# Gate products on centred tokens, with the scale in the eviction, and whole-slab transposes in a sequence layer

## The chip, the cores and the metric

The kernel runs on one core of a Trainium2 chip. The metric is the device time in microseconds (us) of a run. The time before is the median of three runs. The profile is of one further execution.

## The reference

Only what matters is kept. `x` has 2048 tokens of 512 features in bf16.

```python
xn = (x - mean(x)) / sqrt(var(x) + 1e-5)                  # per token
# A: a diagonal complex recurrence over the 2048 tokens
Bu = xn @ B_bar.T                                         # complex, 512 states
h[t] = Lam_bar * h[t-1] + Bu[t]
s = 2 * real(h @ Cmat.T) + xn * Dskip
# B: a gated feed-forward network, F = 1376
g = silu((gelu(xn @ w_gate) * (xn @ w_up)) @ w_down)
out = x + s * g
```

The normalisation divides each token by its own standard deviation. A product with a weight matrix is linear in the token, so `xn @ w` equals `rstd * ((x - mean) @ w)`.

## The kernel before

The tokens go in four slabs of 512, each of four tiles of 128 tokens. All engines run lists that a scheduler in the kernel has ordered beforehand; each engine works its list strictly in order. The order of TensorE for slab 0 is: gate and up products of chunk 0 (384 columns) for the four tiles, chunk 1 (512 columns), the state products of the slab, chunk 2 (480 columns). Then come the state products of slab 1, the down product of slab 0, the gate tiles of slab 1, between them the y tiles of slab 0, and so on.

```python
    # the queue on SyncE, in this order
    load_x(SP, nc.sync, 0, 1.75)
    load_x(SP, nc.sync, 1, 1.9)
    load_first(0, 0, 2.1)            # w_gate chunk 0
    load_x(SP, nc.sync, 2, 2.55)
    load_first(0, 1, 3.1)            # w_up chunk 0
    load_x(SP, nc.sync, 3, 2.9)
    load_first(1, 0, 3.5)            # w_gate, w_up chunk 1
    load_first(1, 1, 3.5)
    dma_first(SP, ...)               # x_tok of slab 1, 512 KB
    for ri, src in enumerate((A_B_re, A_B_im)):      # B, turned on the way
        dma_first(SP, ..., nc.sync.dma_start_transpose(out=BT[:, ri, :, :], in_=src), ...)
    # w_gate, w_up chunk 2, then w_down ...
```

A tile of slab 0 is normalised on VectorE, turned by TensorE into a PSUM bank and evicted. The inverse deviation `rs` comes from a power on GpSimd.

```python
    def norm_dve(s, m):
        V.tensor_scalar(out=xn[m][:], in0=x_tok[:, s * M + m, :],
            scalar1=mv[:, s, m, 0:1], scalar2=rs[:, s, m : m + 1],
            op0=ALU.subtract, op1=ALU.mult)

    def transposed(src, n, dst, reads, writes, bank, evict):
        ...                                     # four T.transpose into ybank[bank]
        if evict == ACT:
            act(out=dst, in_=tp, func=AF.Copy)
        else:
            V.tensor_copy(out=dst, in_=tp)

    def gate_pair(s, m, c, then=((), ()), spare=False):
        ...                                     # one PSUM slot (two banks), or both ybanks
        for bank, (nm, wt) in enumerate((("wg", wg), ("wu", wu))):
            for k in range(KT):
                T.matmul(pss[bank][:, 0:w], lhsT=xnT[:, k, t0 : t0 + P], rhs=wt[:, k, a:b], ...)
        act(out=ud, in_=pss[1][:, 0:w], func=AF.Copy)
        act(out=gd, in_=pss[0][:, 0:w], func=AF.Gelu_apprx_tanh)
        V.tensor_tensor(out=at[j][:, a:b], in0=gd, in1=ud, op=ALU.mult)
```

There are three such slots. ScalarE also loads the table for the sines right after the exponential of `log_dt`, makes the sines and cosines of the rotation tables, and spreads `Dskip` over the partitions (`Drow`).

Slab 1 is normalised on VectorE too, and turned by four DMA transposes of one tile each (`dma_t`). The y tiles multiply states by `C2`, made on VectorE from the turned C matrices, and add the skip term:

```python
    def y_part(s, m, bank, key, a, z, i, e, gi, b, seed):
        if seed:                                # all but the first two y tiles
            act(out=bank, in_=sk[s % 2][:, m, a:z], func=AF.Copy)
        ...                                     # eight matmuls onto the bank
        if seed:
            V.tensor_tensor(out=yg[e][:, a:z], in0=bank, in1=g2[gi][:, b, a:z], op=ALU.mult)
        else:
            V.tensor_tensor(out=ys, in0=bank, in1=sk[s % 2][:, m, :], op=ALU.add)
            V.tensor_tensor(out=yg[e][:], in0=ys, in1=g2[gi][:, b, :], op=ALU.mult)
```

Of the kernel before, what the change touches and what calls it, by code (L numbers as in the profile page):

```python
# [19 lines left out]
LOOK, HOLD, TABLE, ROUNDS, TRIALS = 0.3, 8.0, 6.0, 6, 3000  # L20
# [182 lines left out]
def kernel(  # L203
# [50 lines left out]
    xnT = sb("xnT", [P, KT, 2 * TS])  # L254
# [20 lines left out]
    xn = [sb(f"xn{i}", [P, D]) for i in range(M)]  # L275
# [5 lines left out]
    tF = sb("tF", [P, 2, D], FP32)  # L281
    junk = sb("junk", [P, D])
# [31 lines left out]
    def dma_first(eng, issue, land, emit, writes, **kw):  # L314

        first[eng] = dma(eng, issue, land, emit, writes=writes, after=[first[eng]] if eng in first else (), **kw)
# [29 lines left out]
    dma_first(SP, 1.45, 4.0, lambda: nc.sync.dma_start(out=x_tok[:, M : 2 * M, :], in_=x_r[:, M : 2 * M, :]), [("x", 1, m) for m in range(M)])  # L346
    for ri, src in enumerate((A_B_re, A_B_im)):
        dma_first(SP, 2.4, 4.0, lambda ri=ri, src=src: nc.sync.dma_start_transpose(out=BT[:, ri, :, :], in_=src), [("BT", ri)])
    for which in range(2):
        load_w(dma_first, SP, nc.sync, 2, (1.35, 4.1), which)  # L350
# [21 lines left out]
    def columns():  # L372

        pe(1, 150, lambda: T.matmul(rows, lhsT=pv[0][:], rhs=ident[0 : 2 * NPT, 0 : 2 * NPT], start=True, stop=True),
            [("pv", 0), ("pv", 1), "ident"], [("slot", 2, 0)])
        acts(4, lambda: act(out=dt_, in_=rows[:, 0:NPT], func=AF.Exp), [("slot", 2, 0), "tiny"], ["dt"], table="exp", rank=150.0)
        acts(1, lambda: act(out=tiny[:], in_=zero[:], func=AF.Sin), ["zero", "dt"], ["tiny"], table="silu", rank=150.0)
# [44 lines left out]
    def transposed(src, n, dst, reads, writes, bank, evict):  # L422
        tp = ybank[bank][:].bitcast(BF16)[:, 0:D].rearrange("p (k t) -> p k t", t=P)

        def f():
            for k in range(KT):
                T.transpose(tp[:, k, :], src[:, k * P : (k + 1) * P], ident[:])  # L427
        pe(KT, P, f, reads + ["ident"], [("y", bank)])
        if evict == ACT:
            acts(512, lambda: act(out=dst, in_=tp, func=AF.Copy), [("y", bank)], writes, rank=100.0)  # L430
        else:
            dve(512, lambda: V.tensor_copy(out=dst, in_=tp), [("y", bank)], writes, rate=2.0, rank=40.0)
# [10 lines left out]
    def norm_dve(s, m):  # L443
        dve(512, lambda: V.tensor_scalar(  # L444
            out=xn[m][:], in0=x_tok[:, s * M + m, :], scalar1=mv[:, s, m, 0:1], scalar2=rs[:, s, m : m + 1],
            op0=ALU.subtract, op1=ALU.mult), [("x", s, m), ("mv", s, m), ("rs", s, m)], [("xn", m)], rate=2.0)

# [3 lines left out]
    def dma_t(s, m):  # L451
        c0 = (s % 2) * TS + m * P
        return dma(SP, 1.2, 4.5 if s == 1 else 1.3, lambda: nc.sync.dma_start_transpose(out=xnT[:, :, c0 : c0 + P], in_=xn[m][:]),
            [("xn", m)], turned_tile(s, m))

    def skip(s, m):
        dve(512, lambda: V.tensor_tensor(out=sk[s % 2][:, m, :], in0=xn[m][:], in1=Drow[:], op=ALU.mult),
            [("xn", m), "Drow"], [("sk", s % 2, m)], rate=2.0)
# [4 lines left out]
    def gate_pair(s, m, c, then=((), ()), spare=False):  # L463

        if spare:
            pss, both = [ybank[0][:], ybank[1][:]], [("y", 0), ("y", 1)]
        else:
            i, ps = slot()
            pss, both = [ps[:, 0, :], ps[:, 1, :]], [("slot", i, 0), ("slot", i, 1)]
        a, b = CH0[c]  # L470
        w = b - a
        j = (s * M + m) % NAT
        t0 = (s % 2) * TS + m * P
        q = gu_n[0] % (2 * NGT)
        gu_n[0] += 1
        qb, qo = q // 2, (q % 2) * 512
        for bank, (nm, wt) in enumerate((("wg", wg), ("wu", wu))):
            def f(bank=bank, wt=wt):
                for k in range(KT):
                    T.matmul(pss[bank][:, 0:w], lhsT=xnT[:, k, t0 : t0 + P], rhs=wt[:, k, a:b], start=(k == 0), stop=(k == KT - 1))  # L480
            pe(KT, w, f, turned_tile(s, m) + [(nm, c)], [both[bank]])
            for t in then[bank]:
                t()
        gd, ud = gt[qb][:, qo : qo + w], ub[qb][:, qo : qo + w]
        acts(w, lambda: act(out=ud, in_=pss[1][:, 0:w], func=AF.Copy), both, [("ub", q)])
        acts(w, lambda: act(out=gd, in_=pss[0][:, 0:w], func=AF.Gelu_apprx_tanh), both, [("gt", q)], table="gelu", after=early if c == 0 else (), rank=40.0 if c + m == 0 else 0.0)
        dve(w, lambda: V.tensor_tensor(out=at[j][:, a:b], in0=gd, in1=ud, op=ALU.mult), [("gt", q), ("ub", q)], [("at", j, c)], rate=2.0)

    def gate_tile(s, m):

        j = (s * M + m) % NAT
        t0 = (s % 2) * TS + m * P
# [3 lines left out]
        def mm(ps, bank, wt, c):  # L496
            a, b = CH[c]

            def f():
                for k in range(KT):  # L500
                    T.matmul(ps[:, bank, 0 : b - a], lhsT=xnT[:, k, t0 : t0 + P], rhs=wt[:, k, a:b], start=(k == 0), stop=(k == KT - 1))  # L501
# [51 lines left out]
    def y_tile(s, m):  # L553
        i = y_n[0] % 2
        seed = y_n[0] >= 2
# [7 lines left out]
        for bank, key, a, z in parts:  # L563
            y_part(s, m, bank, key, a, z, i, e, gi, b, seed)

    def y_part(s, m, bank, key, a, z, i, e, gi, b, seed):

        w = z - a
        if seed:
            acts(w, lambda: act(out=bank, in_=sk[s % 2][:, m, a:z], func=AF.Copy), [("sk", s % 2, m)], [key])  # L570

        def f():
            for j in range(2 * NPT):
                T.matmul(bank, lhsT=hst[s % 2][:, j // NPT, j % NPT, m * P : (m + 1) * P], rhs=C2[:, j // NPT, j % NPT, a:z],  # L574
                         start=(j == 0 and not seed), stop=(j == 2 * NPT - 1), skip_group_check=True)
        pe(2 * NPT, w, f, [("hst", s % 2, 0), ("hst", s % 2, 1)] + C2S + ([key] if seed else []), [key])
        if seed:
            dve(w, lambda: V.tensor_tensor(out=yg[e][:, a:z], in0=bank, in1=g2[gi][:, b, a:z], op=ALU.mult),  # L578
                [key, ("g2", gi)], [("yg", e, a)], base=0.13)
        else:  # L580
            ys = tF[:, i, :]
            dve(512, lambda: V.tensor_tensor(out=ys, in0=bank, in1=sk[s % 2][:, m, :], op=ALU.add),
                [key, ("sk", s % 2, m)], [("tF",)], base=0.13)
            dve(512, lambda: V.tensor_tensor(out=yg[e][:], in0=ys, in1=g2[gi][:, b, :], op=ALU.mult),
                [("tF",), ("g2", gi)], [("yg", e, a)], base=0.13)
# [16 lines left out]
    def half(s, h):  # L602
# [3 lines left out]
        for q in range(H2):  # L606
            i, ps = slot()
            pt = h * H2 + q
            for ri in range(2):
                def f(ri=ri, pt=pt, ps=ps):  # L610
                    for k in range(KT):
                        T.matmul(ps[:, ri, :], lhsT=BT[:, ri, k, pt * P : (pt + 1) * P], rhs=xnT[:, k, (s % 2) * TS : (s % 2 + 1) * TS],  # L612
# [61 lines left out]
    def tables():  # L674
# [5 lines left out]
        for f32, lo, pr, n in ((cbt, ch, cp, "c"), (sbt, sh, sp, "s")):  # L680
            pool(0.5, lambda f32=f32, lo=lo: G.tensor_copy(out=lo[:], in_=f32[:, :, 0:NB]), [n + "bt"], [n + "h"])
            acts(128, lambda f32=f32, pr=pr: act(
                out=pr[:], in_=f32[:, :, NB : NB + NA].unsqueeze(3).to_broadcast([P, NPT, NA, 2]), func=AF.Copy), [n + "bt"], [n + "p"], rank=40.0)
# [28 lines left out]
    def head_t(m):  # L712
        transposed(xn[m], m, xnT[:, :, m * P : (m + 1) * P], [("xn", m)], [("xnT", 0, m)], m % 2, DVE if m == 3 else ACT)

    def spread():
        pe(1, 512, lambda: T.matmul(slots[2][:, 1, :], lhsT=warm[0:1, 0:P], rhs=Drow[0:1, :], start=True, stop=True), ["Drow", "warm"], [("slot", 2, 1)])
        acts(512, lambda: act(out=Drow[:], in_=slots[2][:, 1, :], func=AF.Copy), [("slot", 2, 0), ("slot", 2, 1)], ["Drow"])
# [3 lines left out]
    dummies(3, 0)  # L721
# [3 lines left out]
    rstd(0, 0, 1)  # L725
    stats(0, 1)
    mean(0, 1)
    norm_dve(0, 0)
    rstd(0, 1, 2)
    head_t(0)  # L730
    dummies(2, 0, 3)
    turn_angles()
    angle(0)
    norm_dve(0, 1)
    stats(0, 2)
    mean(0, 2)
    rstd(0, 2, 3)
    angle(1)
    stats(0, 3)
    norm_dve(0, 2)  # L740
    mean(0, 3)
    rstd(0, 3, 4)
    angle(2)
    angle(3)
    norm_dve(0, 3)
    pl.in_turn = False
    tables()
    then = {0: ((lambda: head_t(1), spread), ()), 1: ((lambda: head_t(2),), ()), 2: ((lambda: head_t(3),), ())}
    for m in range(M):
        gate_pair(0, m, 0, then.get(m, ((), ())), m == M - 1)  # L750
        if m == 1:
            damping()
    dma_first(SP, 3.6, 4.3, lambda: nc.sync.dma_start(out=wd[:, 0 : NFT - 1, :], in_=B_w_down[0 : (NFT - 1) * P, :].rearrange("(k p) d -> p k d", p=P)), ["wd"])
    dma_first(SP, 0.4, 4.3, lambda: nc.sync.dma_start(out=wd[:FL, NFT - 1, :], in_=B_w_down[(NFT - 1) * P : F, :]), ["wd"])
    for m in range(M):
        skip(0, m)
    for m in range(M):
        gate_pair(0, m, 1)
    for h in range(2):
        half(0, h)  # L760
    for m in range(M):
        gate_pair(0, m, 2)
# [38 lines left out]
    turned = {}  # L801

    def norm_out(s, m):
        acts(512, lambda: act(out=xn[m][:], in_=x_tok[:, s * M + m, :], func=AF.Identity, scale=rs[:, s, m : m + 1], bias=nb[:, s, m : m + 1]),
             [("x", s, m), ("rs", s, m), ("nb", s)], [("xn", m)], ptr=2)
        dma_t(s, m)

    def norm1():
# [4 lines left out]
        for m in range(M):  # L813
            norm_dve(1, m)
            turned[1] = dma_t(1, m)
            skip(1, m)

    def norm_act(s):
        dma(SP, 0.5, 4.0, lambda: nc.sync.dma_start(out=x_tok[:, s * M : (s + 1) * M, :], in_=x_r[:, s * M : (s + 1) * M, :]),
            writes=[("x", s, m) for m in range(M)], not_before=30.0)  # L820
# [19 lines left out]
    for ri, src in enumerate((A_C_re, A_C_im)):  # L840
        dma(SP, 2.4, 5.0, lambda ri=ri, src=src: nc.sync.dma_start_transpose(out=CT[:, ri, :, :], in_=src),
            writes=[("CT", ri)], after=[turned[1]])
# [68 lines left out]
```

## Time and profile before

| what | value |
|---|---|
| time, median of 3 | 181.07 us (181.01 to 181.15) |
| span of the profiled execution | 179.6 us |
| TensorE busy | 97% |
| VectorE busy | 88% |
| ScalarE busy | 65% |
| packets of the main DMA queue, share of 16 engines | 46.3% |
| granted TensorE clock | 0.998 |

A line of the timeline names its start and length in us, the engine, the line of the kernel, the operation, what is written and read, the shape, the count, and in brackets how long the engine sat idle before it and what ended that. "SPq" is SyncE's queue: its length is the time to issue a transfer, not to move the data. Lines of the chain of waits have start, length and what the time went to. One warning: matmuls overlap, so the step from one group to the next says more than a group's own length. A DMA transpose to SBUF counts as a transfer.

### The profile page before, as it was taken

What the parts mean: (1) busy time and instruction counts of PE and PEld (TensorE: products, weight loads), DVE (VectorE), ACT (ScalarE), POOL (GpSimd) and SP (SyncE); (2) the same over time, 40 slices, a digit from 0 to 9 for tenths busy, and PEclk for the clock granted to TensorE, in tenths of its full rate; (3) what the DMA queues carried; (4) which work ended last, traced back from release to release, by engine and by line L of the source; (5) the groups of instructions that cost most, each with busy time, mean ns of one, the idle gap of its engine ahead of it and who ended that gap; (6) DMA issues with size and microseconds to landing.
All of it is one profiled execution on the core that took longest, in us unless ns stands there. A gap on an engine that the chain in (4) does not pass through costs nothing.

```text
span 179.6 us, 2392 instructions
## 1 busy us (share of the span) xinstructions
PE 173.4 (97%) x838; PEld 82.6 (46%) x854; DVE 157.8 (88%) x268; ACT 116.7 (65%) x178; POOL 9.7 (5%) x19
## 2 busy tenths in 40 slices
PE   7999999999999999999999999999999999999992
PEld 2354444444445555444445554544445555444451
DVE  4789999998999999999999999999999999950063
ACT  4788599589999999645359964426618666353220
POOL 3230230000002000000020000000000000000000
PEclk9999999999999999999999999999999999999999
DMA  4999999997000429630011485050100084420011
GB/s 127 332 285 218 367 202 179 305 156 155 0 0 0 80 57 114 130 61 0 0 60 62 93 155 109 1 111 4 58 29 0 2 160 84 82 86 29 0 58 58
DMA packets 47109, 18.01 MB, mean 100 GB/s; under 512 B 38425, under 2 KB 47098, under 8 KB 47098
## 3 DMA queue, kind: packets, MB, share of 16 engines
q1 hardware_dynamic: 47072, 17.86, 46.3%
q8 instruction: 6, 0.10, 0.2%
q14 instruction: 5, 0.04, 0.1%
q10 hardware_dynamic: 26, 0.00, 0.0%
HBM read 6.33 MB, written 2.10 MB: 47 GB/s over the span
## 4 chain that ended last, share of the span: by engine, by line
PE 90%; DMA 4%; DVE 2%; SPq 1%; issue 1%; DVEq 0%
PE slot L501 31%; PE slot L544 21%; PE slot L612 15%; PE ybank L574 13%; PE slot L480 9%; DMA x_tok<-in_A_x_dram 3%; DMA out_dram<-ot 1%; DVE ot L586 1%; PE ybank L480 1%; SPq L328 1%; DVE yg L578 1%; SPq L321 1%; DVE st L402 0%; PE ybank L427 0%; DVE xn L444 0%
## 5 line engine op out<-in xcount | busy, mean ns | idle before, releaser
L501 PEld LDWEIGHTS <-xnT 128*128 128x128 bf16 x288 | 28.2, 98 | 28.4
L544 PE MATMUL slot<-wd,atT 128*128 128x512 bf16 (+1 forms) x173 | 38.5, 379 | 0.2
L501 PE MATMUL slot<-wu,xnT 128*128 128x512 bf16 (+1 forms) x144 | 31.8, 357 | 0.0
L501 PE MATMUL slot<-wg,xnT 128*128 128x512 bf16 (+1 forms) x139 | 31.5, 356 | 0.3
L645 DVE TENSOR_TENSOR_SCAN Fs<-rho,ini,W 128x512 bf16<-128x512 f32 x24 | 29.4, 1269 | 0.0
L612 PE MATMUL slot<-xnT,BT 128*128 128x512 bf16 x124 | 28.1, 379 | 0.2
L574 PE MATMUL ybank<-C,hst 128*128 128x512 bf16 (+1 forms) x125 | 27.6, 372 | 0.2
L544 PEld LDWEIGHTS <-atT 128*128 128x128 bf16 (+1 forms) x176 | 17.2, 98 | 20.9
L615 ACT ACTIVATE U<-slot 128x1024 bf16<-128x1024 f32 x16 | 16.0, 1021 | 12.5 <-PE slot L612 12.5
L578 DVE TENSOR_TENSOR yg<-ybank,g 128x512 bf16<-128x512 f32 (+1 forms) x14 | 9.4, 670 | 12.8 <-PE ybank L574 12.5
L574 PEld LDWEIGHTS <-hst 128*128 128x128 bf16 x136 | 13.3, 98 | 13.8
L612 PEld LDWEIGHTS <-BT 128*128 128x128 bf16 x128 | 12.5, 98 | 15.1
L626 DVE TENSOR_TENSOR Q<-U,tab 128x4096 bf16<-128x4096 bf16 x8 | 18.3, 2289 | 0.2
L626 DVE TENSOR_TENSOR Q<-Fs,tab 128x4096 bf16<-128x4096 bf16 x8 | 18.3, 2289 | 0.1
L548 ACT ACTIVATE g<-slot 128x1024 f32<-128x1024 f32 x8 | 8.2, 1021 | 13.4 <-PE slot L544 13.4
L570 ACT ACTIVATE ybank<-sk 128x512 f32<-128x512 bf16 (+1 forms) x14 | 8.1, 586 | 12.7 <-DVE yg L578 12.0
L509 ACT ACTIVATE gt<-slot 128x1024 bf16<-128x1024 f32 x12 | 12.3, 1023 | 3.7 <-PE slot L501 3.7
L509 ACT ACTIVATE ub<-slot 128x1024 bf16<-128x1024 f32 x12 | 12.2, 1020 | 3.0 <-PE slot L501 2.8
L480 PEld LDWEIGHTS <-xnT 128*128 128x128 bf16 x96 | 9.0, 98 | 9.7 <-ACT xnT L430 0.7
L823 ACT ACTIVATE junk<-x_tok 128x512 bf16<-128x512 bf16 x16 | 10.0, 627 | 1.6 <-DMA x_tok<-in_A_x_dram 1.4
L480 PE MATMUL slot<-wg,xnT 128*128 128x480 bf16 (+2 forms) x43 | 10.4, 360 | 0.4 <-ACT xnT L430 0.4
L480 PE MATMUL slot<-wu,xnT 128*128 128x512 bf16 (+2 forms) x44 | 10.4, 360 | 0.0
(118 smaller groups left out, 179.1 us busy)
## 6 DMA issues: line engine op xcount, KB each, us to landing
out_dram<-ot SPq DMA_DIRECT2D x15, 128.0 KB, 1.7
x_tok<-in_A_x_dram SPq DMA_DIRECT2D x3, 512.0 KB, 5.8
wd<-in_B_w_down_dram SPq DMA_DIRECT2D x1, 1280.0 KB, 9.9
x_tok<-in_A_x_dram SPq DMA_DIRECT2D x4, 128.0 KB, 3.0
wg<-in_B_w_gate_dram SPq DMA_DIRECT2D x1, 512.0 KB
wu<-in_B_w_up_dram SPq DMA_DIRECT2D x1, 512.0 KB, 6.9
wg<-in_B_w_gate_dram SPq DMA_DIRECT2D x1, 480.0 KB, 5.0
wu<-in_B_w_up_dram SPq DMA_DIRECT2D x1, 480.0 KB
```

What stands on the lines that cost most here:

```text
L480: T.matmul(pss[bank][:, 0:w], lhsT=xnT[:, k, t0 : t0 + P], rhs=wt[:, k, a:b], start=(k == 0), stop=(k == KT - 1))
L501: T.matmul(ps[:, bank, 0 : b - a], lhsT=xnT[:, k, t0 : t0 + P], rhs=wt[:, k, a:b], start=(k == 0), stop=(k == KT - 1))
L509: acts(1024, lambda ps=ps, dst=dst, fn=fn: act(out=dst[:, 0:1024].rearrange("p (c w) -> p c w", c=2), in_=ps[:, :, :], func=fn), [("slot", ...
L544: T.matmul(ps[:, b, :], lhsT=atT[:fs, k, m * P : (m + 1) * P], rhs=wd[:fs, k, :], start=(k == 0), stop=(k == NFT - 1))
L548: acts(1024, lambda: act(out=g2[gi][:, :, :], in_=ps[:, :, :], func=AF.Silu), [("slot", i, 0), ("slot", i, 1)], [("g2", gi)], table="silu" ...
L574: T.matmul(bank, lhsT=hst[s % 2][:, j // NPT, j % NPT, m * P : (m + 1) * P], rhs=C2[:, j // NPT, j % NPT, a:z], start=(j == 0 and not seed ...
L578: dve(w, lambda: V.tensor_tensor(out=yg[e][:, a:z], in0=bank, in1=g2[gi][:, b, a:z], op=ALU.mult), [key, ("g2", gi)], [("yg", e, a)], base ...
L612: T.matmul(ps[:, ri, :], lhsT=BT[:, ri, k, pt * P : (pt + 1) * P], rhs=xnT[:, k, (s % 2) * TS : (s % 2 + 1) * TS], start=(k == 0), stop=(k ...
L615: acts(1024, lambda q=q, ps=ps: act(out=U[ui][:, :, q, :], in_=ps[:, :, :], func=AF.Copy), [("slot", i, 0), ("slot", i, 1)], [("U", ui, q)])
L626: dve(4096, lambda: V.tensor_tensor(out=Qf, in0=src.unsqueeze(1).to_broadcast(WQ), in1=table, op=ALU.mult), reads, ["Q"], rate=2.0)
L645: pl.add(DVE, 1.116 if s == 0 else 1.19, lambda ri=ri, q=q, pt=pt, first=first: V.tensor_tensor_scan(out=Fs[:, ri, q, :], data0=rho[:, pt ...
L823: acts(512, lambda i=i, fn=fn, m=m: act(out=junk[:], in_=x_tok[:, s * M + m, :], func=fn, accum_out=sx[:, s, i, m : m + 1]), [("x", s, m)] ...
```

## The change

In chunks 0 and 1 of slab 0 the products take tokens less their mean, not divided by their deviation. ScalarE multiplies by the deviation's inverse as it evicts the gate and up banks. So the transposes of the first tiles need not wait for the power on GpSimd. The normalised tokens of slab 0 are still made, for the states, chunk 2 and the skip term, and a DMA turns the four tiles at once. Slab 1 is also turned by one DMA. The token tile is now laid out by tile and then by feature block.

```diff
-    xnT = sb("xnT", [P, KT, 2 * TS])
+    xnT = [sb(f"xnT{i}", [P, M, KT, P]) for i in range(2)]
...
+    xc = [Fs[:, i // 2, i % 2, :] for i in range(M)]
+    xcT = W[:].rearrange(...)                  # turned, centred tokens
...
+    def turn_slab(s, land, after=()):
+        return dma(SP, 2.0, land, lambda: nc.sync.dma_start_transpose(
+            out=xnT[s % 2][:].rearrange("p m k t -> p (m k) t"), in_=xn_all[:].rearrange("p m d -> p (m d)")), ...)
...
+    def center(m):
+        dve(512, lambda: V.tensor_scalar(out=xc[m], in0=x_tok[:, m, :], scalar1=mv[:, 0, m, 0:1], scalar2=None, op0=ALU.subtract), ...)
...
+            if self.bare:                      # chunks 0 and 1 of slab 0
+                kw, rd, ptr = dict(scale=rs[:, 0, m : m + 1]), [("rs", 0, m)], 1
+            acts(w, lambda: act(out=ud, in_=pss[1][:, 0:w], func=AF.Copy, **kw), ...)
+            acts(w, lambda: act(out=gd, in_=pss[0][:, 0:w], func=AF.Gelu_apprx_tanh, **kw), ...)
```

TensorE turns the first two tiles before its first product, and the table for the sines is loaded after their two evictions:

```diff
+    head_t(0, ACT)
+    dummies(2, 0)
+    behind = [head_t(1, ACT)]
+    acts(1, lambda: act(out=tiny[:], in_=zero[:], func=AF.Sin), ..., after=behind)
+    tables()
+    pairs = [GatePair(m, 0, m == M - 1) for m in range(M)]
+    pairs[0].products(0)
+    spread()
+    pairs[1].products(0)
+    pairs[0].products(1)
+    head_t(2, ACT)
...
```

The queue after chunk 1 of the weights is now: B (two transposes), slab 0 turned, x of slab 1, chunk 2 of the weights, C (real part), slab 1 turned, w_down, the first two tiles of the gated activations, C (imaginary part), x of slab 2. Before, it was: x of slab 1, B, chunk 2 of the weights, w_down, slab 1 turned in four, C (both), x of slabs 2 and 3.

The skip term is seeded by ScalarE for every y tile, the first two with it, so the branch without a seed falls away. The scheduler tries more orders (8000, not 3000), so the lists differ in small things throughout.

## The prediction

> **What bounds the kernel now.** I read the page's busy times first, then the chain of waits in order of time, then the timeline of the first 14 us, and last the timelines of single engines round every place where TensorE could come to wait. The page:
>
> ```profile
> PE 173.4 (97%) x838; PEld 82.6 (46%) x854; DVE 157.8 (88%) x268; ACT 116.7 (65%) x178; POOL 9.7 (5%) x19
> ```
>
> TensorE is busy nearly all the time and VectorE is the next engine. The chain of waits (start, us, what) shows where TensorE is not yet or not wholly fed:
>
> ```profile
> 3.23 5.05 DMA x_tok<-in_A_x_dram
> 8.28 0.02 issue
> 8.30 0.69 DVE st L402
> 8.99 0.32 DVE xn L444
> ...
> 9.36 0.40 PE ybank L427 x4
> ...
> 13.84 6.64 PE slot L480 x30
> ```
>
> From 13.84 on the chain holds only TensorE (in pieces with 0.05 us of issue between them) to 172.59, where the last store follows. Before it lies the arrival of the fourth token tile. So the change, which adds no product and removes none (the real matmuls of both programs are the same, only two warm-up matmuls fewer), can gain only before 13.4 us, and lose anywhere. The timeline there (start, us, engine):
>
> ```profile
> 2.85 0.69 DVE L402 BATCH_NORM_STATS2 st<-x_tok 128x6 f32<-128x512 bf16 x1 [1.71 <-DMA x_tok<-in_A_x_dram]
> 3.58 0.18 DVE L406 BATCH_NORM_AGGREGATE mv<-st 128x2 f32<-128x6 f32 x1
> ...
> 4.03 0.57 POOL L409 TENSOR_TENSOR rs<-ve,mhalf 128x1 f32<-128x1 f32 x1 [1.98 <-DVE ve L412]
> ...
> 4.68 0.38 DVE L444 TENSOR_SCALAR xn<-x_tok,mv,rs 128x512 bf16<-128x512 bf16 x1
> ...
> 5.55 0.60 ACT L430 ACTIVATE xnT<-ybank 128x512 bf16<-128x512 bf16 x1
> ...
> 6.21 0.82 PE L480 MATMUL slot<-wg,xnT 128*128 128x384 bf16 x4 [0.36 <-ACT xnT L430]
> ...
> 8.30 0.69 DVE L402 BATCH_NORM_STATS2 st<-x_tok 128x6 f32<-128x512 bf16 x1 [0.90 <-DMA x_tok<-in_A_x_dram]
> ...
> 11.01 1.28 ACT L486 ACT_TABLE_LOAD   x1
> ...
> 12.30 0.49 ACT L486 ACTIVATE gt<-slot 128x384 bf16<-128x384 f32 x1
> ...
> 13.41 1.03 PE L480 MATMUL slot<-wg,xnT 128*128 128x512 bf16 x3
> ```
>
> The first product starts at 6.21 and the second chunk of the gate at 13.41: 7.20 us. The eight groups of four 384-column matmuls need 8 x 0.65 = 5.2 (0.65 is the step from one group to the next), four transposes of a tile 4 x 0.22, the Drow spread and the small lambda product about 0.3. That is 6.3; some 0.8 us is gaps, the largest of 0.55 before the transposes at 9.36.
>
> **What the skill says.** "ScalarE: Activation LUTs", section "What ACT_TABLE_LOAD costs", gives about 1283 ns for a table load and about 93 ns more for each [128,1] pointer operand. The trace has 1.28 us; the 93 ns cannot be seen on a gate eviction before the change, for its scale is immediate. "VectorE: DVE Perf Modes", "The perf-mode tier table", lets a bf16 tensor_scalar run faster than a tensor_tensor; at 512 elements here they take 0.38 and 0.42 us, and I charge a centring 0.38. "DMA: Bandwidth & Descriptors", "Latency and other measured facts", gives 261 GB/s for a DMA transpose; 512 KB would take 2.0 us, which agrees with the queue's time for the second B matrix below. The same page, "Queues, rings and completion order", says each DMA engine consumes its ring in order, so a load behind a transpose waits for it.
>
> **The change in the head, step by step.** The first tile's statistics end at 3.76 as before. The centring starts at 3.80 in place of the normalisation's 4.68, as it needs no GpSimd power: 0.88 us earlier. Its transpose starts at about 4.27 (one dummy instead of three lets TensorE be free), and ScalarE evicts at 4.70 to 5.30. This works since the sine table load (4.14 to 5.42 before) is now behind the second eviction. The second tile: statistics from 4.10, centring 5.05 to 5.45, transpose at 5.50, eviction 5.93 to 6.53. TensorE's order is now two transposes, then products, so the first product starts at about 5.72: 0.5 us earlier than 6.21. Then spread, gate of tile 1 (6.6), up of tile 0 (its weights were there by 7.50 before; I put 7.4), transposes of tile 2 at 8.05, up of tile 1 to 8.92.
>
> Now ScalarE: table load 6.54 to 7.82, tiny sine, Drow 7.95, eviction of tile 2 from 8.47 to 9.07. The lambda product waits for that bank, so tile 2's gate starts at 9.2, a gap of 0.3. The fourth tile's statistics start at 8.3, as before, for x_tok lands then; but VectorE's queue is shorter there, and its centring ends at 9.6 where the normalised tile came at 10.9. Transposes at 9.85, up of tile 2 to 10.72. The eviction on VectorE is behind the first real normalisation: 10.28 to 10.70, about on time. Tile 3's two groups end at 12.05. ScalarE must by then have freed slot 0: sines and copies 9.0 to 9.95, the first scaled eviction to 10.45, gelu's table to 11.73, gelu to about 12.3. So the second chunk starts at about 12.3, not 13.41: **1.1 us earlier**, held by ScalarE and no longer by the tokens. Sixteen scaled evictions at 0.093 add 1.5 us of ScalarE work, but each has a 0.65 or 0.87 us group per bank to hide under.
>
> **The queue.** The transposes of B and the slabs:
>
> ```profile
> 5.58 6.79 SPq L348 DMA_TRANSPOSE BT<-in_A_B_re_dram  x1
> 12.42 1.98 SPq L348 DMA_TRANSPOSE BT<-in_A_B_im_dram  x1
> ...
> 19.88 5.92 SPq L453 DMA_TRANSPOSE xnT<-xn  x4
> ```
>
> [...] 512 KB less ahead (the slab 1 load moves back) at the page's 330 GB/s is 1.5 us. So B's two issues end at about 10.9 and 12.9. The new whole-slab transpose is 512 KB too: issued 12.9 to 14.9, as the last xn is ready at about 11.7; it lands some 2.4 us later (B lands 9.2 after its issue, 2.4 after the issue's end): 17.3. It is needed by the state products at 12.3 + 8 x 0.865 = 19.2. Slack 1.9. The x load of slab 1, issued at 15, waits for this transpose and lands at about 19. VectorE wants it at about 19.5: on the edge. The slab 1 transpose is issued at 26, lands at 30, needed at 32.6; the down weights behind it land at about 35, needed at 39.5 (40.61 less 1.1).
>
> **VectorE, the second limit.** It gets four centrings (1.3 us at a step of 0.33) and loses two additions of the first y tiles, 0.69 each, whose skip term ScalarE now seeds, and two tiny rstd steps. The sum is about nil, but the cost comes early and the gain after 66 us. I have the first table product at 13.85 instead of 13.10, and the rotation of the first states at about 26.9 instead of 26.59. The places where VectorE reaches TensorE later:
>
> ```profile
> 61.67 0.75 DVE L849 SCALAR_TENSOR_TENSOR C<-hst,ncre,tF 128x512 bf16<-128x512 bf16 x1
> ...
> 72.54 0.67 DVE L582 TENSOR_TENSOR tF<-ybank,sk 128x512 f32<-128x512 f32 x1
> ```
>
> The last C2 tile ends at 62.42 and the first y tile starts at 64.07: 1.6 us of slack. The fourth y tile needs its bank read (72.54 to 73.21) and seeded by ScalarE (73.24 to 73.84), and starts at 70.44 + 2 x 1.73 = 73.90: no slack at all. With TensorE 1.1 us ahead this read must come at 71.45. In the new order 9.44 us of VectorE work lie between the rotation that starts at 62.33 now and this read, against 10.21 now. The stretch before it, 35.74 now, loses 0.6 of small steps that go later and up to 0.67 of idle, and gains 0.25: some 34.7 to 35.4. So 26.9 + 35.0 + 9.4 = 71.3, if slab 1 is there in time. Most of the 1.1 us is kept; I take off 0.25 for this edge and small waits.
>
> Sum: 181.07 - 1.1 + 0.25 = **180.2 us**.
>
> **The rivals.** First: VectorE takes the place of the tokens. If slab 1's load lands at 21 instead of 19 (x loads take 5.8 us from issue to landing on this page, which from 15 gives 20.8), VectorE stands still 1 to 1.5 us and so does the fourth y tile: all of the gain is gone, 181.0 to 181.5. VectorE's 88% and its full tenths from 18 to 150 us speak for it; against it, the two additions that fall away. Second: the whole-slab transpose is late. A tile of 128 KB takes 2.7 us to land, four in one should take about 4.4; if it took 7 it would land at 20 and the state products would wait 0.8: 181.0. Third: ScalarE's sines, table and scaled evictions hold slot 0 longer than 12.3; each tenth is a tenth of the end. At 13.0 the gain is 0.4: 180.7. Fourth: nothing holds and the head is ended by the tokens alone, at 12.05: 179.7.
>
> **Range and chances.** From 179.7 (the fourth) to 181.2 (the first at half weight). No path yields 2% (3.6 us): the head has 1.35 to give at most. A loss of 3.6 us would need a load that misses by more than any slack above: 2%.
>
> **What would show it.** The centring near 3.8 and the first product near 5.7; the gelu of slot 0 ending at 12.3 and the second chunk right behind; no idle before the state products near 19.2, nor before VectorE's statistics of slab 1; the fourth y tile right behind the third. A wait on a DMA in the state, down or statistics steps makes the prediction wrong, as does a first chunk that again ends after 13 us, or slower state products from the token layout, which is now in runs of 128.

## The result and the profile after

| | kernel before | changed kernel |
|---|---|---|
| median | 181.03 us (180.86 to 181.15, 6 runs) | 182.25 us (181.70 to 182.63, 6 runs) |
| ratio | 1 | 1.0066 (95% interval 1.0047 to 1.0085) |
| profiled execution: span | 179.6 us | 179.9 us |

The change costs 0.7%. The profiled execution of the changed kernel is the best of its six (181.70 us), and that of the kernel before (181.37 us) took longer than any of its six. So the two traces hold only 0.33 us of the loss; the experiments come back to the spread of the runs. First the page's busy times of the changed kernel:

```profile
PE 173.5 (96%) x838; PEld 82.5 (46%) x852; DVE 157.8 (88%) x268; ACT 120.1 (67%) x180; POOL 9.6 (5%) x17
```

TensorE's and VectorE's work is what it was; ScalarE has 3.4 us more. So the two busiest engines have no more work than before: something waits. The timeline of the head, the part that answers to the one shown of before:

```profile
3.74 0.35 DVE L466 TENSOR_SCALAR Fs<-x_tok,mv 128x512 bf16<-128x512 bf16 x1
...
5.59 0.81 PE L501 MATMUL slot<-wg,W 128*128 128x384 bf16 x4
...
8.23 0.69 DVE L420 BATCH_NORM_STATS2 st<-x_tok 128x6 f32<-128x512 bf16 x1
...
10.46 1.28 ACT L514 ACT_TABLE_LOAD   x1
...
11.75 1.05 ACT L514 ACTIVATE gt<-slot,rs 128x384 bf16<-128x384 f32 x2
...
12.39 1.02 PE L501 MATMUL slot<-wg,W 128*128 128x512 bf16 x3 [0.22 <-ACT gt L514]
```

The second gate chunk starts at 12.39, not 13.41, and what ends its wait is ScalarE's gelu, no longer the tokens. The head gives 1.02 us. Following TensorE's groups shows where they go:

| start of the group on TensorE | before | after | difference |
|---|---|---|---|
| second gate chunk | 13.41 | 12.39 | -1.02 |
| state products, slab 1 | 33.71 | 32.68 | -1.03 |
| down product, slab 0 | 40.61 | 39.58 | -1.03 |
| gate tiles of slab 1 after it | 50.13 | 49.29 | -0.84 |
| second y tile of slab 0 | 70.44 | 69.60 | -0.84 |
| state products, slab 2 | 75.62 | 75.99 | +0.37 |
| last y tile | 168.96 | 169.33 | +0.37 |

In the kernel before, the second, third and fourth y tiles follow one another at 1.73 us each. So the fourth should start at 69.60 + 2 x 1.73 = 73.06 and starts at 73.83. In all, 0.19 goes within the down product, 0.77 before the fourth y tile, 0.44 before slab 2's states; then nothing more is lost. From the second y tile to slab 2's states it is 6.39 us where the kernel before takes 5.18; this stretch serves as a measure below. The chain of waits (start, us, what) tells what is behind the last two:

```profile
35.94 2.50 SPq L362
...
38.50 4.50 DMA x_tok<-in_A_x_dram
...
43.02 0.73 ACT junk L863 x2
...
65.88 0.61 ACT ybank L596
...
66.55 1.86 POOL rs L427
...
68.43 0.17 DVE nb L874
...
68.63 2.93 ACT xn L843 x4
71.56 0.90 ACT ub L537
...
73.33 2.52 DMA xnT<-xn
...
75.99 1.02 PE slot L631 x4
```

Before, the chain held only TensorE from 13.84 on. Now it goes through the load of slab 2's tokens, the passes that sum them (`junk`), GpSimd's power, the bias `nb`, four normalisations and a transpose. In the kernel before, two steps of the same path stood thus in the timeline:

```profile
30.56 1.13 SPq L819 DMA_DIRECT2D x_tok<-in_A_x_dram  x2
...
56.84 1.32 POOL L409 TENSOR_TENSOR rs<-sx,mhalf 128x4 f32<-128x4 f32 x1 [29.48 <-ACT gt L517]
```

The load is issued 7.9 us later (38.50 against 30.56), the power comes 9.7 us later (66.55 against 56.84): all that slack is gone. The timeline of the changed kernel round the loss:

```profile
66.31 1.22 DVE L657 TENSOR_TENSOR W<-Q 128x2048 bf16<-128x2048 bf16 x1
66.55 1.85 POOL L427 TENSOR_TENSOR rs<-sx,mhalf 128x4 f32<-128x4 f32 x1 [35.57 <-ACT ybank L596]
68.43 0.17 DVE L874 SCALAR_TENSOR_TENSOR nb<-sx,rs 128x4 f32<-128x4 f32 x1 [0.90 <-POOL rs L427]
68.63 2.93 ACT L843 ACTIVATE xn<-x_tok,nb,rs 128x512 bf16<-128x512 bf16 x4 [0.73 <-DVE nb L874]
72.47 0.67 DVE L603 TENSOR_TENSOR yg<-ybank,g 128x512 bf16<-128x512 f32 x1
73.17 0.60 ACT L596 ACTIVATE ybank<-sk 128x512 f32<-128x512 bf16 x1 [0.36 <-DVE yg L603]
73.83 1.89 PE L600 MATMUL ybank<-C,hst 128*128 128x512 bf16 x8 [0.61 <-ACT ybank L596]
75.99 2.32 PE L631 MATMUL slot<-xnT,BT 128*128 128x512 bf16 x10 [0.28 <-DMA xnT<-xn]
```

VectorE works its list in order, so while `nb` waits 0.90 for the power, the read of the bank behind it waits too, then ScalarE's seed of that bank, then the fourth y tile. And the four normalisations, 2.93 us of ScalarE, end so late that the turned tokens land at 75.85. The lengths of the two-input addition `W<-Q` and of the power beside it matter again below.

### The profile page after: what moved, and what is told of

Its sections match the earlier page's. It is cut to its first block, busy times and chain, and to the rows that moved or that the text cites. A ratio compares the mean times of both kernels' runs of the same rounds, so it can differ in the third digit from the quotient of the medians.

```text
span 179.9 us, 2385 instructions
## 1 busy us (share of the span) xinstructions
PE 173.5 (96%) x838; PEld 82.5 (46%) x852; DVE 157.8 (88%) x268; ACT 120.1 (67%) x180; POOL 9.6 (5%) x17
## 4 chain that ended last, share of the span: by engine, by line
PE 68%; DVE 10%; DMA 7%; ACT 6%; SPq 3%; issue 2%; POOL 1%; DVEq 0%
PE slot L529 28%; PE slot L572 19%; PE ybank L600 11%; PE slot L631 8%; DMA x_tok<-in_A_x_dram 5%; PE slot L437 2%; SPq L555 2%; ACT xn L843 2%; DMA xnT<-xn 1%; SPq L362 1%; DVE st L420 1%; DVE at L516 1%; DVE Q L645 1%; DVE Q L712 1%; POOL rs L427 1%
## 5 line engine op out<-in xcount | busy, mean ns | idle before, releaser
L529 PEld LDWEIGHTS <-xnT 128*128 128x128 bf16 x288 | 28.2, 98 | 28.4
L603 DVE TENSOR_TENSOR yg<-ybank,g 128x512 bf16<-128x512 f32 (+1 forms) x16 | 10.6, 669 | 12.9 <-PE ybank L600 12.7
L596 ACT ACTIVATE ybank<-sk 128x512 f32<-128x512 bf16 (+1 forms) x16 | 9.2, 586 | 11.8 <-DVE yg L603 11.7
L664 DVE TENSOR_TENSOR_SCAN Fs<-rho,W 128x512 bf16<-128x512 f32 x8 | 9.3, 1211 | 0.0
L501 PEld LDWEIGHTS <-W 128*128 128x128 bf16 x64 | 5.8, 97 | 6.0 <-issue 0.4
L547 DVE TENSOR_TENSOR at<-gt,ub 128x1024 bf16<-128x1024 bf16 x12 | 8.2, 683 | 0.1
```

Source lines behind the costliest of these rows:

```text
L529: T.matmul(ps[:, bank, 0 : b - a], lhsT=xnT[s % 2][:, m, k, :], rhs=wt[:, k, a:b], start=(k == 0), stop=(k == KT - 1))
L547: dve(1024, lambda: V.tensor_tensor(out=at[j][:, 0:1024], in0=gt[q][:, 0:1024], in1=ub[q][:, 0:1024], op=ALU.mult), qs[0] + qs[1], [("at", ...
L664: pl.add(DVE, 1.116 if s == 0 else 1.19, lambda ri=ri, q=q, pt=pt, first=first: V.tensor_tensor_scan(out=Fs[:, ri, q, :], data0=rho[:, pt ...
```

## The experiments

Theory N: the load of slab 2 stands last in the new queue order, so slab 2's normalisation reaches VectorE and ScalarE when the y tiles need them, and its wait is passed on. Some edits below move steps in the scheduler's finished lists; a number is the place in its time, and a tag names the step.

**The changed kernel, unchanged** (`again`).

> The changed kernel once more, unchanged, to see where its runs differ. Theory N (slab 2's normalisation ends too late): a longer run has the same start of the state products at 19.3 us and a longer wait at the fourth y tile or at the state products of slab 2. Rival D (transfers that land late in other places): the extra time of a longer run sits at the down product of slab 0 or before 35 us. Time 181.7 to 182.6 in either case.

182.22 us, ratio 1.0063 (1.0038 to 1.0088). TensorE waited 0.60 before the fourth y tile and 0.26 before slab 2's states, as above (0.61 and 0.28), and 0.33 in the down product. From the second y tile to slab 2's states it was 6.36. So this part of the loss repeats, but theory N's longer wait did not come: the execution took 0.42 longer than the one above, and TensorE's groups put 0.12 of it in the head (second chunk at 12.51) and 0.30 in the down product. So the difference between the two sits where rival D had it, in the down product and before 35 us.

**Only the load goes ahead** (`x_early`).

```diff
+    ('load', 2): 31.75,      # in the queue: behind w_down, ahead of the turned activations
```

> The load of slab 2's tokens goes from behind the imaginary part of C to right behind the down weights, in every list all else keeps its place. Rival L (the late landing itself, 43.0 us, makes the normalisation late): statistics and all that follows come earlier, the fourth y tile and the state products of slab 2 do not wait, time 0.8 to 1.2 us below the changed kernel, about 181.2. Theory N (the place of the eight statistics passes in ScalarE's list makes it late): the last pass still ends near 65.5, both waits stay, time within 0.3 us of the changed kernel.

182.14 us, ratio 1.0045 (1.0028 to 1.0063). The load is issued at 30.17, and the down product waits no more. But ScalarE's last summing pass still ends at 66.26, and the two other waits are as before, for the lists behind the load kept their order:

```profile
68.89 0.16 DVE L885 SCALAR_TENSOR_TENSOR nb<-sx,rs 128x4 f32<-128x4 f32 x1 [0.90 <-POOL rs L438]
...
74.28 1.89 PE L611 MATMUL ybank<-C,hst 128*128 128x512 bf16 x8 [0.61 <-ACT ybank L607]
```

A new wait of 0.33 came at 54.39, behind a wait of 1.6 of ScalarE for the imaginary part of C, which is now issued later (38.05). So for this path, data that lie there early help nothing while an in-order list asks for them late.

**The load and the whole normalisation go ahead** (`norm_early`).

```diff
+    ('load', 2): 31.75, ('sum', 2, 0): 37.5, ... ('sum', 2, 7): 55.2,
+    ('var', 2): 57.25, ('pow', 2): 57.6, ('nb', 2): 59.48,
+    ('xn', 2, 0): 61.94, ... ('xn', 2, 3): 65.14, ('turn', 2, 0): 62.8, ...
```

> Load of slab 2 as in x_early, and its eight statistics passes, the variance, the bias step and the four normalisations also moved forward in the lists of ScalarE and VectorE, about to where the kernel before has them. Work and all other places unchanged. Theory N: no wait of TensorE at the fourth y tile nor at the state products of slab 2, these start at 74.6 to 75.0 (75.99 in the changed kernel), time 180.0 to 180.5. Rival V (VectorE's added work alone makes the fourth y tile late): that wait of 0.6 stays, time 180.8 to 182.

181.19 us, ratio 1.0004 (0.9988 to 1.0019): 1.0 us of the loss is back. On TensorE's timeline the y tiles and the state products now follow without a wait:

```profile
70.35 5.34 PE L631 MATMUL ybank<-C,hst 128*128 128x512 bf16 x23
75.53 2.75 PE L662 MATMUL slot<-xnT,BT 128*128 128x512 bf16 x12
```

The stretch from the second y tile to slab 2's states is back at 5.18, so theory N holds and rival V (VectorE's added work alone) does not. The time and the states' start at 75.53 lie outside theory N's ranges all the same. In this execution the head came 0.43 later than in the changed kernel (second chunk at 12.82), and the step to the gate tile at 54.69 is 0.51 too long, behind a wait of 0.9 of ScalarE for the imaginary part of C. Without the two the states would start at 74.6.

**The bias on GpSimd** (`bias_on_gpsimd`), so that VectorE's list no longer holds the waiting step.

```diff
-            V.tensor_scalar(out=mean, in0=mean, scalar1=1.0 / D, ...)
+            V.tensor_scalar(out=mean, in0=mean, scalar1=-1.0 / D, ...)
-        dve(M, lambda: V.scalar_tensor_tensor(out=nb[:, s, :], in0=mean, scalar=-1.0, in1=rs[:, s, :], ...
+        dve(M, lambda: G.tensor_tensor(out=nb[:, s, :], in0=mean, in1=rs[:, s, :], op=ALU.mult),
```

> The changed kernel, but the small step that makes the bias of slab 2's normalisation is done by GpSimd, so VectorE does not stand 0.9 us in its list behind the power. Rival V: the fourth y tile's wait was all that counted; it falls from 0.6 to nothing and the time falls by 0.5 to 0.8 us. Theory N: the fourth y tile no longer waits, but the state products of slab 2 still start near 76.0 to 76.3, as the turned tokens land no earlier; time within 0.3 us of the changed kernel.

182.36 us, ratio 1.0088 (1.0052 to 1.0123): both theories had the fourth y tile without a wait, and it waits. VectorE's wait of 0.90 is gone, but ScalarE's list has the seed behind the normalisations:

```profile
70.11 2.93 ACT L843 ACTIVATE xn<-x_tok,nb,rs 128x512 bf16<-128x512 bf16 x4 [1.26 <-POOL nb L874]
...
74.83 1.89 PE L600 MATMUL ybank<-C,hst 128*128 128x512 bf16 x8 [0.67 <-ACT ybank L596]
```

Two lists carry the wait to the same tile; freeing one leaves the other. Slab 2's states start at 77.47, later than expected too: this execution lost 0.84 more in the down product, and the stretch from the second y tile to the states grew to 6.92, with a bias that now takes 0.66 on GpSimd and not 0.17.

**The scheduler knows of a slower power** (`replan`).

```diff
+    def power(out, base, exponent, n, reads, writes, slow=0.0):
+        pool(0.45 + 0.2 * n + slow, ...)
-        power(rs[:, s, :], var, mhalf[:], M, ...)
+        power(rs[:, s, :], var, mhalf[:], M, ..., slow=1.0)
```

> The changed kernel, only the scheduler's estimate of the GpSimd power for slabs 2 and 3 raised by 1.0 us, so that all lists are ordered again. Theory Z (the order left no slack in slab 2's normalisation, and the power took 0.6 longer than the scheduler assumed): the waits before the fourth y tile and slab 2's state products shrink to under half of 0.9 together: 181.3 to 181.8. Rival (the queue's place of slab 2's load alone decides): it is still last, the waits stay, 182.0 to 182.5.

186.46 us, ratio 1.0302 (1.0284 to 1.0319): far outside both. The new search put slab 2's load behind all four turned activations, issued at 41.28, and ScalarE's list holds the summing passes ahead of the down product's eviction `g`:

```profile
47.23 0.63 ACT L863 ACTIVATE junk<-x_tok 128x512 bf16<-128x512 bf16 x1 [4.02 <-DMA x_tok<-in_A_x_dram]
...
52.61 1.89 PE L529 MATMUL slot<-wu,xnT 128*128 128x512 bf16 x8 [1.27 <-ACT g L576]
```

ScalarE stands 4.02 us for the late load and TensorE pays at 52.61, 55.16 and 57.50 (1.27, 0.67 and 0.98). A wait of 1.42 follows before slab 2's states, so theory Z's waits did not shrink. A load late in the queue passed on by an in-order list is the same kind of cause, in another place and stronger. The scheduler counts 4.0 us from issue to landing for this load; here it was 47.2 - 41.28 = 5.9.

**The head with normalised tokens** (`norm_head`): chunks 0 and 1 lose the centring and the scaled evictions, and the power is made tile by tile; the rest of the change stays.

```diff
-        ... scalar1=mv[:, 0, m, 0:1], scalar2=None, op0=ALU.subtract)
+        ... scalar1=mv[:, 0, m, 0:1], scalar2=rs[:, 0, m : m + 1], op0=ALU.subtract, op1=ALU.mult)
-                kw, rd, ptr = dict(scale=rs[:, 0, m : m + 1]), [("rs", 0, m)], 1
```

> The changed kernel, but chunks 0 and 1 of slab 0 multiply normalised tokens again, with plain evictions; the two transposes ahead of the first product, the late table load, the queue and the whole-slab transposes stay. If the centring (no wait for the power) makes the head's gain: the first tile's transpose waits for the power, the second chunk starts at 13.2 to 14 instead of 12.4, and the time is 183 to 184. Rival (ScalarE's list ends the head, the tokens' wait lies beside it): the second chunk starts within 0.3 of 12.4 and the time is within 0.4 of the changed kernel's 182.2.

184.39 us, ratio 1.0187 (1.0157 to 1.0216). The first tile waits for the power again and the second chunk comes at 14.01; it and the time lie a little beyond what was expected:

```profile
3.91 0.58 POOL L427 TENSOR_TENSOR rs<-ve,mhalf 128x1 f32<-128x1 f32 x1 [1.96 <-DVE ve L430]
...
4.56 0.38 DVE L466 TENSOR_SCALAR Fs<-x_tok,mv,rs 128x512 bf16<-128x512 bf16 x1
...
14.01 1.03 PE L501 MATMUL slot<-wg,W 128*128 128x512 bf16 x3
```

So in the new order the centring is worth 14.01 - 12.39 = 1.62, and the new order without it is 0.60 worse than the old one. The lists behind it were ordered anew, so the total is not the centring's alone.

**The whole gain, first try** (`best1`): as `norm_early`, earlier still, with the load and the imaginary C in the queue's pause behind the real C.

```diff
+QUEUE = {('load', 2): 20.5, ('C', 1): 20.6}
+    ('sum', 2, 0): 33.43, ... ('var', 2): 52.3, ('nb', 2): 56.63, ...
```

> The changed kernel with slab 2's load and the imaginary part of C issued in the queue's pause behind the real part of C (before slab 1's turn), and slab 2's eight statistics passes, its variance, power and bias made 13 to 18 us earlier. Theory N (the loss is slab 2's normalisation chain, whose load stood last in the queue, plus transfers in one crowded queue): no wait before the second half of slab 0's down product, none of 0.3 before the fourth y tile or slab 2's state products, and the second gate chunk near 12.4; the whole gain of the head stays: 180.0 to 180.4. Rival Q (the queue has no room: what goes ahead only moves the wait): slab 1's state products or the down product then wait for their transfers, and the time stays at 181.2 or more.

180.71 us, ratio 0.9984 (0.9976 to 0.9992), between the two expectations: the waits of theory N are gone (5.18 from the second y tile to the states), but rival Q has a part. Slab 1's turn is issued at 28.68 instead of 25.81, and its state products start at 33.11, which is 6.81 after the gate chunk before them starts, where it was 6.48 in the changed kernel:

```profile
33.11 7.08 PE L672 MATMUL slot<-xnT,BT 128*128 128x512 bf16 x32 [0.16 <-DMA xnT<-xn]
```

**The table copies behind the first gelu evictions** (`best2`).

```diff
+    ('pair', 'c'): 12.21, ('pair', 's'): 12.22,
```

> As the run before it here, and the two 0.2 us copies of the rotation table on ScalarE go behind the first two gelu evictions. Theory S (ScalarE's list holds slot 0 at 12.3, as the prediction said): the second gate chunk starts 0.3 to 0.4 earlier, at 12.0 to 12.1, and the time is 0.3 below the run before it. Rival: TensorE's own first chunk ends near 12.05 and VectorE's table products, which read these copies at 13.9, come later and pass the lateness on: less than 0.15 or nothing.

180.71 us (179.98 to 181.07), ratio 0.9976 (0.9967 to 0.9986): no gain in the median. In this execution the second chunk came at 12.76, not at 12.0 to 12.1, and TensorE's timeline says why the head did not profit:

```profile
4.73 1.06 PE L480 MATMUL slot<-junk 128*128 128x512 bf16 x2
...
6.01 1.14 PE L544 MATMUL slot<-wg,W 128*128 128x384 bf16 x4
```

The first product took 1.14 where it took 0.81 in the changed kernel, and two warm-up matmuls 1.06 where `best1` took 0.59: TensorE ran at about half its rate until past 6 us. "TensorE: Matmul & The Clock Gate", "Part 1: The HAM clock gate (the "warmup" mystery)", says that TensorE starts at half rate and is released after a window of activity that runs free of the kernel's start, so that the moment varies from run to run. The traces agree: with the first warm-up at 1.04 or 1.05 in every trace, the warm-up matmul at 3.84 was at full rate in `best1` (0.39), while products at 6 us were not in `best2`. The early head of the change puts real work into that stretch.

**The imaginary C behind w_down** (`best3`).

```diff
-    ('C', 1): 20.6,
+    ('C', 1): 32.05,
```

> The version with all of slab 2's normalisation early and the table copies behind the first gelu evictions, but the imaginary part of C goes behind the down weights instead of ahead of slab 1's turn. Theory Q (that transfer, 4.0 us of issue, pushed slab 1's turn from 25.8 to 28.7 and so its state products by 0.3): these follow slab 0's without a wait and the median comes to 180.2 to 180.4, 0.3 to 0.5 below the 180.71 of the version before. Rival: the turn's landing time hardly depends on it, or the imaginary C is now late for VectorE's C2 and something waits near 54: 180.6 or more.

180.44 us, ratio 0.9963 (0.9950 to 0.9976), just above theory Q's range and below its rival's 180.6; the interval overlaps that of `best2`, so the timeline says more than the time. The turn is issued at 25.87 again and TensorE's timeline has no wait in the stages in question:

```profile
5.61 0.81 PE L544 MATMUL slot<-wg,W 128*128 128x384 bf16 x4
...
12.02 1.03 PE L544 MATMUL slot<-wg,W 128*128 128x512 bf16 x4
...
32.31 7.07 PE L674 MATMUL slot<-xnT,BT 128*128 128x512 bf16 x32
```

In this execution the second chunk starts at 12.02, right behind TensorE's own first chunk (11.37 + 0.65): ScalarE no longer holds it, and it is 0.37 earlier than in the changed kernel, as theory S had it for `best2`. Its span is 178.4, 1.2 below that of the kernel before.

**One warm-up matmul less** (`best4`).

```diff
-    dummies(2, 0)
+    dummies(1, 0)
```

> As the run before it here, with one warm-up matmul instead of two between the first two transposes of tokens. Theory W (the head's spread is TensorE's half clock, left at another moment from 3.9 to 7 us in each run: while it lasts a warm-up matmul of 512 columns takes 0.43 and the second transpose comes late): in runs that leave it late the first product comes 0.3 to 0.4 earlier, in the others nothing changes; the median is 0.1 to 0.2 lower. Rival (the idle time left there keeps the clock low for longer): the median is the same or up to 0.3 higher.

180.44 us, ratio 0.9965 (0.9951 to 0.9978): the same. The profiled executions of both left the half clock by about 5 us, so theory W was not put to its test; it stays open.

**The power with no two-input VectorE operation under way** (`power_free`).

```diff
+    ('yg', 0, 0, 0): 66.0,      # on VectorE: behind the variance's four small steps
```

> The changed kernel; on VectorE alone the product of the first seeded y tile goes behind the four small steps of slab 2's variance instead of ahead of them, so that it, with one input in PSUM, and not the 1.22 us addition with two inputs in SBUF, has begun when GpSimd's power starts. Theory P (the power of 1.85 us is a power of 1.0 that is held until VectorE's two-input addition ends, 0.86 before its own end): it takes 1.0 to 1.1, the bias no longer waits 0.9 for it, the fourth y tile waits 0.2 to 0.4 instead of 0.6, and the time is 0.2 to 0.4 below the changed kernel's 182.2, as ScalarE's four normalisations can start only behind a gelu eviction. Rival (the power's length has nothing to do with VectorE): it stays at 1.85 and the waits stay.

182.11 us (180.86 to 183.34, 16 runs), ratio 1.0052 (1.0031 to 1.0073). The timeline settles the power's length:

```profile
65.82 0.68 DVE L614 TENSOR_TENSOR yg<-ybank,g 128x512 bf16<-128x512 f32 x1
66.05 1.01 POOL L438 TENSOR_TENSOR rs<-sx,mhalf 128x4 f32<-128x4 f32 x1 [34.69 <-ACT junk L874]
66.42 1.21 DVE L668 TENSOR_TENSOR W<-Q 128x2048 bf16<-128x2048 bf16 x1
...
67.56 0.15 DVE L885 SCALAR_TENSOR_TENSOR nb<-sx,rs 128x4 f32<-128x4 f32 x1
...
75.89 7.07 PE L642 MATMUL slot<-xnT,BT 128*128 128x512 bf16 x32 [0.52 <-DMA xnT<-xn]
```

The same power takes 1.01 instead of 1.85, the bias waits for nothing, and the fourth y tile follows the third at once. Slab 2's states still wait 0.52, as the four normalisations start only 0.4 earlier; the stretch from the second y tile to them takes 5.87. In the median this is 0.1, less than expected and far less than the runs' spread. "SBUF — State Buffer", "Who interferes with whom", says that a VectorE operation with two inputs in SBUF contends with a GpSimd operation that reads SBUF for a shared read interface, that the order of issue decides which of the two blocks, and that a VectorE operation with at most one SBUF input doesn't contend outside the two-port modes. The traces agree for a power that comes second: in the changed kernel the addition with two SBUF inputs ends at 66.31 + 1.22 = 67.53 and the power at 68.40, 0.87 later; here, beside a product with one input in PSUM, it is not held. They do not show the other order: here the addition starts 0.37 after the power, before the power's end, and still takes 1.21.

## Why the prediction was wrong

- **The head, step by step: right.** Centring 3.74 (3.80 predicted), first product 5.59 (5.72), fourth statistics 8.23 (8.3), the slot's gelu done at 12.34 (12.3), second chunk 12.39 (12.3), held by ScalarE as said. The gain is 1.02, not 1.1, in the profiled execution. `norm_head` shows that the gain needs the centring.
- **The queue as far as it was followed: right.** Slab 0's turn issued by 15.78 (14.9), in time for the states at 19.29 without a wait; slab 1's load landed at 19.85 (19), and VectorE's statistics began at 19.88. This edge was as thin as the prediction said: VectorE stood about 0.1 there, and 0.5 to 0.6 in the traces of `x_early`, `replan` and `best3`. No run isolates how much of the load's 4.03 is a wait for the transpose ahead of it. The 2.0 us for 512 KB was set beside a time to issue: slab 0's whole turn took 2.88 to issue, slab 1's 1.90 to issue and 4.4 to land, the 4.4 that the second rival counts. So the first rival was not what happened, nor the second; the third and fourth concern the head alone. The new token layout did not slow the state products (7.07 for a slab, as before).
- **VectorE up to the y tiles: right.** First rotation 27.02 (26.9), the rotation behind C2 at 61.98 (26.9 + 35.0 = 61.9).
- **The step that failed** is the sentence "In the new order 9.44 us of VectorE work lie between the rotation that starts at 62.33 now and this read". It took 72.47 - 61.98 = 10.49, and 0.90 of the excess of 1.05 is the wait for GpSimd's power. The step counted VectorE's work and took its list to be ready; the "0.6 of small steps that go later" were seen to move, and were slab 2's variance and bias, which carry that wait. The queue's working stopped at the down weights. The text before the prediction lists slab 2's load as the last of the queue, behind C, but the working never asks who needs it. The rivals had a load that comes late, but slab 1's.
- **What that step was worth:** 0.77 at the fourth y tile and 0.44 at slab 2's states, which no step foresaw. `norm_early` takes both away by moving this path, and its median is 1.0 lower; against `x_early`, which has the early load alone, it is 0.95 lower. `power_free` takes the 0.77 away by letting the power run free. The prediction's own sign of being wrong, a wait on a DMA in the state or down steps, is what the trace shows.
- **"I take off 0.25 for this edge and small waits": too small.** The down product's wait for turned activations, behind C in the queue, made it longer by 0.19 in the profiled execution, 0.49 in `again` and 1.03 in `bias_on_gpsimd`, but by nothing in `power_free`, with the same queue. Where the centring is kept and the table copies stay ahead of the gelu, the second chunk came at 12.39 to 12.55 in the executions that reached the full clock by about 5 us, at 12.82 and 12.96 in `norm_early` and `replan`, which reached it later, and at 13.00 in `power_free`, where the first up product waited 0.33 for its weights. The changed kernel's two sets of runs span 1.55 us (181.64 to 183.19), two larger sets of the kernel before, of 38 and 23 runs, 0.58 and 1.02 (180.77 to 181.35 and 180.84 to 181.86). How the spread divides between clock and transfers was not settled.
- **The range** ended at 181.2 because the worst rival (181.0 to 181.5, taken at half weight) took little more than the gain away. That a wait outside the head could cost more than the head gives was in none of them.

The idea of the change was sound: with slab 2's path and one transfer moved and the table copies behind the gelu, the kernel of `best3` is 0.37% faster than the one before.

## What to carry to other kernels

When a change reorders a queue, follow every load that moved back to its consumer, through each in-order list it passes, down to the engine that sets the end; most of all the last one. A count of an engine's work between two points is a lower bound: ask of each small step in it whom it waits for. And free a waiting path in all lists at once, since one list left behind (ScalarE's seed in `bias_on_gpsimd`, the unmoved sums in `x_early`) keeps the whole wait.

## What the hardware showed unasked

- Slab 2's GpSimd power of 128x4 took 1.01 us in `power_free`, 1.32 in the kernel before, 1.85 in the changed kernel and 2.92 in `best1`. Each of the three longer ones started 0.23 or 0.24 us after a VectorE operation with two SBUF inputs and ended 0.86 to 0.87 after that operation's end: a product of 0.69 us gives 1.32, an addition of 1.22 gives 1.85, a product of 2.29 gives 2.92.
- One transposing transfer of 512 KB holds its queue for very different times: the turn of slab 1 was issued in 1.84 us in `best1` and 2.97 in `best3`, the imaginary C in 2.50 in the changed kernel and 5.35 in `best3`. The transfers ahead of it differed each time; no run isolates what sets the length.
- With a scale from a [128,1] pointer the 384-column evictions of the up product took 0.57 us, not 0.49.
